# The loads of v for seven of eight batches move from SyncE's queue to GpSimd's

## The chip, the cores and the metric

The kernel runs on one core of one Trainium2 chip. Its time is the device time of one execution in microseconds (us), the median of several. Engines are called as in the profile: PE is TensorE (PEld its loading of weights), DVE is VectorE, ACT is ScalarE, POOL is GpSimd and SP is SyncE. PEq, SPq and so on are the sequencers of these engines, which issue DMAs and wait for semaphores.

## The reference

For each of 8 batches there are u and v (3200 x 256) and z (3200 x 64), all float32:

```
scores = (z @ z.T) / 3200
x      = u * (max(scores, 0)**2 @ v)
gate   = sigmoid(causal 5-tap convolution of x along the rows, one filter per column)
out    = (gate * (x @ w_val)) @ w_out
```

The scores are 3200 x 3200 per batch and symmetric. The weights w_val and w_out (256 x 256) and the taps (5 x 256) come as 64-bit floats and are made into 32-bit ones by the kernel.

## The kernel before

**Precision.** TensorE works in float32r. Each factor is split into a high and a low part, and a product is three matmuls: low x high, high x low, high x high. v too is split: `v_high` (line 410) casts a loaded piece, on ScalarE for all batches but the first, and `v_low` (line 415) subtracts the high part from the loaded piece on DVE. Both parts go to tiles `v_hl0` to `v_hl12`, one for each pair of row tiles (the 25 tiles of 128 rows make 12 pairs and a single). Each of these has one buffer, so the parts for a batch are written as the batch before has used them for the last time.

**Order of the work.** A batch (b = 0 to 7) is cut into six chunks of 512 query rows, and a remainder of 128 rows that is handled beside the sixth chunk (c = 5). For a chunk, 13 steps run over the pairs of key tiles; the sixth has 16, three of them for the remainder. A step's `scores` are computed three steps ahead of their use (AHEAD = 3). `weights_of` then makes the step's weights: ScalarE applies relu (line 640) and square (641) and casts the high part `ah` (643), DVE subtracts for the low part `al` (649). `attend` multiplies them with v on TensorE (line 428, tiles `acc`). Because the scores are symmetric, many blocks are not computed twice: DVE turns a finished block into a tile `turned` (520, 530), `keep` (542) stores it to DRAM as `mir`, and `m_fetch` (551, 555) loads it later as `m`, six steps before its use. Such a step needs no scores; ScalarE only casts `m` to `ah`.

**What sets the order.** The order is written out by hand. A function is hung on a step by `at_step`, and the instructions of each engine run in just the order in which the program emits them. An engine starts each as soon as its semaphores allow, and may be several steps ahead of another engine. An engine's DMAs stand in that engine's order too: a DMA that waits for its buffer holds up everything behind it on the engine that issues it. On SyncE each DMA waits also for an earlier one, as its eight completion semaphores go round.

**The loads of v.** `v_rows` issues four DMAs, one for each 32-partition block, for up to four neighbouring row tiles; `v_load` calls it. For b > 0, the list `V_LOAD` says at which step of the last chunk of the batch before which tiles are loaded, and into which buffer:

```
V_LOAD = (
    (2, (0, 1, 2, 3), (0, 0)), (3, (24,), (1, 6)), (4, (4, 5, 6, 7), (0, 4)),
    (6, (8, 9, 10, 11), (1, 0)), (8, (12, 13), (1, 4)), (10, (20, 21, 22, 23), None),
    (12, (14, 15, 16, 17), None), (16, (18, 19), None),
)
```

The third item is a place in one of two `v_raws` tiles, which share the two buffers of `turned`; `None` means a `v_raw` tile of a ring of two. Tiles 14 to 17 need two calls of `v_rows`, so a batch has nine groups of four DMAs. In this text the row-24 group is the second, which loads the single tile 24, and the ninth group is the one at step 16, tiles 18 and 19; step 16 is the first step of the next batch. The ninth group takes the `v_raw` buffer of tiles 20 to 23, and so must wait until `v_low` of the pair 22, 23 has read it. `V_HIGH` names the step at which each pair is cast; the pair 18, 19 comes last, two steps after its load is issued.

**GpSimd's own work.** It sets or copies the four rows that the convolution needs from the chunk before (`x_halo`, lines 766 and 768), keeps the last four of a chunk (`halo_keep`, 774 and 779), and has a few instructions for the remainder rows (`one_mul`, 1048, and others). These are small and lie between the places where v is loaded.

**The end.** After the last step the remainder of the last batches and the last chunk are finished, TensorE waits there for other engines in turn.

Of the kernel before, what the change touches and what calls it, by code (L numbers as in the profile page):

```python
# [17 lines left out]
def attn_glu_kernel(  # L18
# [29 lines left out]
    nc = tc.nc  # L48
# [303 lines left out]
    def v_rows(dst, b, g, t, m):  # L352

        for a in range(P // BLK):
            k = firsts[g] * P + (a * sizes[g] + t) * BLK
            nc.sync.dma_start(  # L356
                dst[a * BLK : (a + 1) * BLK], v[b, k : k + m * BLK, :].rearrange("(t r) d -> r t d", r=BLK)
            )

    def v_load(b, tiles_, into=None):  # L360


        raw = sb.tile([P, CW // P, D], F32, name="v_raw", bufs=2) if into is None else into
        for j, k in enumerate(tiles_):
            v_raw[b, k] = raw, j
        j = 0
        while j < len(tiles_):
            g, t = homes[tiles_[j]]
            m = 1
            while j + m < len(tiles_) and homes[tiles_[j + m]] == (g, t + m):  # L370
                m += 1
            v_rows(raw[:, j : j + m], b, g, t, m)
            j += m
# [1048 lines left out]
    with tc.manual_schedule():  # L1422
# [13 lines left out]
        for s in range(min(todo), END + 1):  # L1436
            b, c, i = steps[s] if s >= 0 else (0, 0, 0)
# [85 lines left out]
            if s == END:  # L1523

                b, c = LAST
# [93 lines left out]
```

## Time and profile before

| | |
|---|---|
| median of 3 runs | 2260.3 us (2259.65 to 2263.69) |
| the profiled execution's own time | 2260.35 us |
| its span | 2258.3 us |
| granted TensorE clock | 1.00 |
| busy: PE / PEld / DVE / ACT / POOL | 2247.2 / 1943.2 / 1851.7 / 1702.5 / 75.5 us |
| mean DMA traffic | 171 GB/s |
| DMA issues on line 356 (v loads) | 288 |

The span is the time from the first to the last instruction that the profile shows; the execution's time is a little longer. An engine's busy time is the time covered by its instructions. Register work, semaphore waits and issuing of DMAs are not in it. The chain that ended last is followed back from the last instruction, at each step to what released it. A row of waits names who waited, for whom, and then the total, the number of times and the longest. A row of the timeline starts with its start and its length in us, and ends with the idle time of the engine ahead of it and what ended that.

### The profile page before, as it was taken

How to read it: one execution, taken by the hardware profiler on the slowest of the kernel's cores; microseconds unless marked ns; L12 is line 12 of the kernel's file. 1: busy time of each engine (PE TensorE's matmuls, PEld its weight loads, DVE VectorE, ACT ScalarE, POOL GpSimd, SP SyncE). 2: the span in 40 equal slices, each digit the busy share in tenths (PEclk: the TensorE clock that was granted, in tenths of full speed). 3: DMA queues.
4: the chain of work that ended last, by engine and by line, in shares of the span. 5: the costliest groups of instructions: out<-in, count | busy, mean ns of one | idle time of the engine just before them, and what ended most of it. 6: DMA issues, size and time to landing. Idle time of an engine off the chain costs nothing.

```text
span 2258.3 us, 49991 instructions
## 1 busy us (share of the span) xinstructions
PE 2247.2 (100%) x20269; PEld 1943.2 (86%) x20269; DVE 1851.7 (82%) x2292; ACT 1702.5 (75%) x2126; POOL 75.5 (3%) x116
## 2 busy tenths in 40 slices
PE   9999999999999999999999999999999999999998
PEld 7888988889888998888988899888898889988887
DVE  8877788877889778887888868888788887888776
ACT  8987698766887668876598766977669776687753
POOL 0000000000000000000000000000000000000000
PEclk9999999999999999999999999999999999999999
DMA  5556967878677785787767777678777787777672
GB/s 126 118 136 149 211 153 163 191 180 209 150 167 180 187 205 141 177 189 189 180 162 169 186 188 178 160 178 186 187 176 176 166 187 187 176 175 165 168 184 91
DMA packets 700567, 386.59 MB, mean 171 GB/s; under 512 B 411824, under 2 KB 635056, under 8 KB 700336
## 3 DMA queue, kind: packets, MB, share of 16 engines
q1 hardware_dynamic: 699008, 383.01, 71.9%
q8 instruction: 158, 2.59, 0.5%
q14 instruction: 73, 0.60, 0.1%
q10 hardware_dynamic: 1328, 0.39, 0.1%
HBM read 211.82 MB, written 171.44 MB: 170 GB/s over the span
## 4 chain that ended last, share of the span: by engine, by line
PE 95%; DMA 2%; DVE 1%; SPq 1%; issue 1%; ACT 1%; DVEq 0%; ACTq 0%
PE acc L428 69%; PE s L428 13%; PE misc L428 11%; DMA m<-mir 1%; PE acc L725 1%; DVE al L649 1%; SPq L356 1%; DMA v_raws<-in_v_dram 0%; ACT ah L643 0%; SPq L1008 0%; PE misc L435 0%; DVE x L756 0%; SPq L555 0%; PE acc L936 0%; PE misc L936 0%
## 5 line engine op out<-in xcount | busy, mean ns | idle before, releaser
L428 PE MATMUL acc<-ah,v_hl 64*128 64x512 f32 x9472 | 1622.1, 388 | 1.4 <-DVE x L756 0.5
L428 PEld LDWEIGHTS acc<-ah,v_hl 64*128 64x128 f32 x9472 | 967.9, 184 | 148.7 <-issue 2.1
L428 PE MATMUL acc<-al,v_hl 64*128 64x512 f32 x4736 | 979.7, 387 | 1.2 <-DVE al L649 1.1
L428 PEld LDWEIGHTS acc<-al,v_hl 64*128 64x128 f32 x4736 | 496.3, 184 | 73.6 <-DVE al L649 3.2
L649 DVE TENSOR_TENSOR al<-a,ah 128x1024 fp32r<-128x1024 f32 (+1 forms) x346 | 397.0, 1148 | 185.1 <-ACT ah L643 183.4
L640 ACT ACTIVATE a<-s 128x1024 f32<-128x1024 f32 (+1 forms) x346 | 333.2, 963 | 143.5 <-PE s L428 127.9
L643 ACT CAST ah<-m 128x1024 fp32r<-128x1024 f32 x254 | 265.0, 1047 | 141.9 <-PE acc L428 98.4
L641 ACT ACTIVATE a<-a 128x1024 f32<-128x1024 f32 (+1 forms) x346 | 347.7, 1005 | 11.0
L649 DVE TENSOR_TENSOR al<-m,ah 128x1024 fp32r<-128x1024 f32 x254 | 307.5, 1211 | 45.9 <-ACT ah L643 43.4
L643 ACT CAST ah<-a 128x1024 fp32r<-128x1024 f32 (+1 forms) x323 | 319.9, 990 | 10.2
L520 DVE STREAM_TRANSPOSE turned<-a 128x1024 f32<-128x1024 f32 (+1 forms) x278 | 318.4, 1145 | 0.1
L807 DVE SCALAR_TENSOR_TENSOR gate<-x,cw,gate 128x512 f32<-128x512 f32 x384 | 282.4, 735 | 3.6
L428 PE MATMUL s<-zq,zhl 64*128 64x512 f32 (+1 forms) x1596 | 222.8, 378 | 0.2 <-DVE gv L1029 0.2
L428 PEld LDWEIGHTS s<-zq,zhl 64*128 64x128 f32 x1596 | 154.1, 184 | 27.4 <-DVE gv L1029 0.6
L756 DVE TENSOR_TENSOR x<-acc,ut 128x512 f32<-128x512 f32 x96 | 61.9, 686 | 84.8 <-PE acc L428 70.9
L812 ACT ACTIVATE gate<-gate 128x512 f32<-128x512 f32 x96 | 60.6, 631 | 68.2 <-DVE gate L807 68.0
L877 ACT CAST gvh<-gv 128x512 fp32r<-128x512 f32 x96 | 59.4, 620 | 41.4 <-DVE gv L873 41.3
L428 PE MATMUL misc<-xh,w_val_lo 64*128 64x512 f32 x376 | 79.2, 386 | 0.0
L428 PE MATMUL misc<-xl,w_val_hi 64*128 64x512 f32 x376 | 79.2, 386 | 0.0
L428 PE MATMUL misc<-xh,w_val_hi 64*128 64x512 f32 x376 | 79.2, 386 | 0.0
L428 PE MATMUL s<-v_hl,ah 64*128 64x512 f32 x400 | 77.1, 394 | 0.0
L873 DVE TENSOR_TENSOR gv<-misc,gate 128x512 f32<-128x512 f32 x94 | 64.5, 686 | 15.1 <-PE misc L428 10.8
(175 smaller groups left out, 2023.6 us busy)
## 6 DMA issues: line engine op xcount, KB each, us to landing
mir<-turned SPq DMA_DIRECT2D x460, 256.0 KB, 4.1
m<-mir SPq DMA_DIRECT2D x230, 512.0 KB, 4.8
u_raw<-in_u_dram SPq DMA_DIRECT2D x384, 64.0 KB, 3.6
mir<-turned SPq DMA_DIRECT2D x376, 64.0 KB, 2.1
m<-mir SPq DMA_DIRECT2D x94, 256.0 KB, 4.3
out_dram<-ob SPq DMA_DIRECT2D x152, 128.0 KB, 3.1
v_raws<-in_v_dram SPq DMA_DIRECT2D x100, 128.0 KB, 3.8
z_raw<-in_z_dram SPq DMA_DIRECT2D x182, 64.0 KB, 3.2
```

What stands on the lines that cost most here:

```text
L356: nc.sync.dma_start(dst[a * BLK : (a + 1) * BLK], v[b, k : k + m * BLK, :].rearrange("(t r) d -> r t d", r=BLK))
L428: ins = nc.tensor.matmul(out_, st[r], mv[r], start=first, stop=last)
L520: nc.vector.transpose(into[:, t : t + m], a[:, j * w : (j + m) * w].rearrange("p (t m x) -> p t m x", t=m, x=BLK))
L640: nc.scalar.activation(a[:, : n * w].rearrange("p (j x) -> p j x", j=2), s[:, :, :each], AF.Relu, scale=scale)
L641: nc.scalar.activation(a, a, AF.Square)
L643: nc.scalar.copy(hi, a)
L649: nc.vector.tensor_tensor(lo, a, f32(hi), op=ALU.subtract)
L756: nc.vector.tensor_tensor(x[:, h, HALO : HALO + w], accs[b, c][h][:, :w], ut[b, c][:, h, :w], op=ALU.mult)
L807: nc.vector.scalar_tensor_tensor(g, tap, cw[:, h, k : k + 1], g, op0=ALU.mult, op1=ALU.add)
L812: nc.scalar.activation(g, g, AF.Sigmoid)
L873: nc.vector.tensor_tensor(gv[:, :w], pvs[b, c][e][:, :w], gates[b, c][:, e, :w], op=ALU.mult)
L877: nc.scalar.copy(gvs[b, c][0][:, e, :w], gv_[b, c, e][:, :w])
```

## The change

For b > 0 the DMAs of `v_rows` are issued by GpSimd, for b = 0 by SyncE as before. Their places in the program, their sources, their buffers and their sizes stay. There are 4 x 9 of them for each of 7 batches.

```
     def v_rows(dst, b, g, t, m):
 
         for a in range(P // BLK):
             k = firsts[g] * P + (a * sizes[g] + t) * BLK
-            nc.sync.dma_start(
+            (nc.gpsimd if b else nc.sync).dma_start(
                 dst[a * BLK : (a + 1) * BLK], v[b, k : k + m * BLK, :].rearrange("(t r) d -> r t d", r=BLK)
             )
```

More of the change, by code (lines that the diff above doesn't have):

```diff
@@ L355, in v_rows @@
             k = firsts[g] * P + (a * sizes[g] + t) * BLK
-            nc.sync.dma_start(
+            (nc.gpsimd if b else nc.sync).dma_start(
                 dst[a * BLK : (a + 1) * BLK], v[b, k : k + m * BLK, :].rearrange("(t r) d -> r t d", r=BLK)
```

## The prediction

> **What bounds the kernel now.** I read the page's head first, then the span in three stretches, then who waits for whom, then the chain through the one place where TensorE stood still. First the page:
>
> ```profile
> span 2258.3 us, 49991 instructions
> ...
> PE 2247.2 (100%) x20269; PEld 1943.2 (86%) x20269; DVE 1851.7 (82%) x2292; ACT 1702.5 (75%) x2126; POOL 75.5 (3%) x116
> ...
> PE 95%; DMA 2%; DVE 1%; SPq 1%; issue 1%; ACT 1%; DVEq 0%; ACTq 0%
> ```
>
> TensorE is busy for 2247.2 of 2258.3 us and carries 95% of the chain that ended last. Where the missing 11.1 us lie decides what any change off TensorE can give. The stretches (columns: length, then busy time and count by engine, granted clock, DMA share, GB/s):
>
> ```profile
> 0.00:15.00 15.00, 13.06 (x73) 9.03 (x75) 9.92 (x18) 9.26 (x14) 1.32 (x10) 1.00 0.63 136
> 15.00:2220.00 2205.00, 2202.00 (x20018) 1907.54 (x20016) 1817.13 (x2226) 1681.64 (x2087) 72.31 (x102) 1.00 0.74 174
> 2220.00:2258.30 38.30, 32.17 (x184) 26.62 (x180) 24.66 (x50) 11.56 (x26) 1.86 (x4) 0.99 0.14 45
> ```
>
> 1.9 us are lost at the start and 6.1 at the end, where no moved load lies (the first batch keeps SyncE, and nothing is loaded for a ninth). Between them TensorE idles for 2205.00 - 2202.00 = 3.0 us, at full clock. So 3.0 us is the most that this change can win; a loss has no such bound.
>
> Who waits around the moved loads (waiting engine, line, released by: total, times, longest):
>
> ```profile
> ACT ah L643 <- DMA m<-mir: 36.9, 28, 4.7
> ACT v_hl L410 <- DMA v_raws<-in_v_dram: 24.8, 7, 4.6
> SPq L356 <- DVE v_hl L415: 48.7, 7, 8.2
> ```
>
> ScalarE waits once per moved batch for a v load, 24.8/7 = 3.5 us, and 28 times for a mirrored block. SyncE stands 48.7/7 = 7.0 us per batch before the last group of a batch (rows 18 and 19), whose buffer DVE has still to read. None of this reaches TensorE except in one place, at b = 4, where the chain reads (start, length, what):
>
> ```profile
> 1103.09 0.43 SPq L356
> ...
> 1103.62 6.46 DMA m<-mir
> ...
> 1110.15 1.05 ACT ah L643
> ...
> 1111.23 1.24 DVE al L649
> ...
> 1112.51 0.49 PE acc L428
> ```
>
> A mirrored block is fetched only after four v loads have been issued (L356). It lands 6.46 us later, ScalarE and DVE split it, and TensorE gets it late.
>
> **The change, part by part.** 36 DMAs per batch, 252 in all, move from SyncE's queue to GpSimd's. Bytes, buffers and the steps of the program stay.
>
> *Removed from SyncE.* The price of an issue there, by tile (min/median/max in ns):
>
> ```profile
> L356 SPq DMA_DIRECT2D v_raws<-in_v_dram x156: 311/430/2107, 14.3 to 1944.6; - x156
> L356 SPq DMA_DIRECT2D v_raw<-in_v_dram x132: 311/426/1932, 3.1 to 1970.2; - x132
> ```
>
> 252 x 0.43 = 108 us of issue time leave SyncE, off TensorE's path nearly everywhere. What counts is the issue just ahead of the late fetch at b = 4, and the same place at b = 5:
>
> ```profile
> 1100.97 2.55 SPq L356 DMA_DIRECT2D v_raws<-in_v_dram  x4
> 1103.62 1.20 SPq L555 DMA_DIRECT2D m<-mir  x2
> ...
> PE acc L428 <- DVE al L649: 0.8, 1, 0.8
> PE acc L428 <- ACT ah L643: 0.5, 1, 0.5
> ...
> PE acc L428 <- DVE al L649: 0.3, 1, 0.3
> ```
>
> The first two rows are SyncE's timeline: four v loads fill 2.55 us straight ahead of the fetch. The others are TensorE's waits from 1050 to 1130 us, 0.8 + 0.5 = 1.3, and from 1360 to 1411 us, 0.3. A fetch 2.6 us earlier covers both, if its transfer is as long as before: **-1.6 us**. If the transfer grows by what the issue saves: 0. I take -1.6, since the wait sits behind an issue, and keep 0 and -3.0 as ends. SyncE's 7.0 us standing per batch moves to GpSimd too. Behind it on SyncE lie stores of turned blocks and of the output, which no engine awaits there, so I count nothing.
>
> *Added to GpSimd: the price of one issue.* No row of this trace shows a DMA issued by GpSimd. The nearest rows are SyncE's 0.43 us above and GpSimd's own instructions (first row grouped by line: busy, mean ns; the second min/median/max):
>
> ```profile
> L1048 POOL TENSOR_TENSOR one_sum<-one_sum,one_f 128x512 f32<-128x512 f32 (+1 forms) x4 | 6.4, 1594 | 122.4 <-DMA one_f<-in_u_dram 122.4
> L774 POOL COPY halo<-x x40: 191/1052/1219, 56.0 to 2189.7; 128x8 f32<-128x8 f32 x40
> ```
>
> Ends: 0.43 and 1.59 us. A copy of eight elements has a median of 1.05 us, so I take g = 1.05 us as an estimate, nearer to GpSimd's rows than to SyncE's. GpSimd has 75.5 us of work in 2258.3; 252 x 1.05 = 265 us more fit by far. What matters is when a group lands.
>
> *The first eight groups of a batch* (32 DMAs). On SyncE they stand in line; on GpSimd only their buffers hold them. At b = 2, SyncE, then ScalarE's first use:
>
> ```profile
> 520.16 1.77 SPq L542 DMA_DIRECT2D mir<-turned  x4
> ...
> 528.08 2.71 SPq L356 DMA_DIRECT2D v_raws<-in_v_dram  x4
> ...
> 532.92 2.01 SPq L356 DMA_DIRECT2D v_raws<-in_v_dram  x4
> ...
> 536.67 0.41 ACT L410 CAST v_hl<-v_raws 128x256 fp32r<-128x256 f32 x1 [2.97 <-DMA v_raws<-in_v_dram]
> ...
> 575.73 0.63 ACT L410 CAST v_hl<-v_raw 128x512 fp32r<-128x512 f32 x1
> ```
>
> The second buffer is free when the stores issued up to 521.9 have landed, about 2 us on, near 524, and the row-24 group, from 532.92 on SyncE, can start there: 9 us earlier. The first v wait of ScalarE goes, 3.0 us here. At g = 1.05 it ends near 524 + 4.2 + 2 = 530; even at 1.59, near 532.4, it beats 536.67. The 28 DMAs from there on end near 524 + 29.4 + 2 = 555 at g = 1.05, near 571 at 1.59; the last of these eight groups is first used at 575.73. TensorE does not wait at this place, so nothing is counted.
>
> *The ninth group* (rows 18 and 19) is the place that decides. Its buffer comes free at the same moment on either queue, and ScalarE uses it soon after. b = 2 (SyncE, ScalarE, DVE's remainder of the next block, TensorE's first use of it), then the time to landing of these four, then b = 1:
>
> ```profile
> 574.27 1.73 SPq L356 DMA_DIRECT2D v_raw<-in_v_dram  x4
> 580.50 0.63 ACT L410 CAST v_hl<-v_raw 128x512 fp32r<-128x512 f32 x1
> 584.27 1.23 DVE L649 TENSOR_TENSOR al<-a,ah 128x1024 fp32r<-128x1024 f32 x1 [1.16 <-ACT ah L643]
> 586.46 0.39 PE L428 MATMUL acc<-al,v_hl 64*128 64x512 f32 x2
> ...
> DMA to landing us min/median/max: 1.8/1.9/2.1
> ...
> 303.30 2.42 SPq L356 DMA_DIRECT2D v_raw<-in_v_dram  x4
> 308.38 0.61 ACT L410 CAST v_hl<-v_raw 128x512 fp32r<-128x512 f32 x1
> 308.51 1.23 DVE L649 TENSOR_TENSOR al<-a,ah 128x1024 fp32r<-128x1024 f32 x1 [1.17 <-ACT ah L643]
> 310.69 0.39 PE L428 MATMUL acc<-al,v_hl 64*128 64x512 f32 x2
> ```
>
> The block is paired with its use by counting writes and uses in program order. On GpSimd the fourth DMA starts 3g after the first and lands g - 0.43 + 2.1 later, so the group is in 4g + 1.67 us after its buffer is free. At b = 2 ScalarE comes 580.50 - 574.27 = 6.23 us after that, at b = 1 5.08 us. Lateness: 4g - 4.56 and 4g - 3.41. ScalarE's next work is the block that TensorE takes with 586.46 - 585.50 = 0.96 us to spare (585.50 is 584.27 + 1.23; 0.95 at b = 1), its thinnest margin in that chunk. With g = 1.05 the group is in time at b = 2 and 0.79 us late at b = 1, less than 0.95: **0 us**. b = 3 to 7 repeat b = 2 nearly to the tenth. At g = 1.59, b = 2 is 1.80 us late, which is the first rival.
>
> *Queued behind the waiting issue on GpSimd* are the halo copy of the last chunk (L779), a memset of x (L766) and a product (L1048). They start up to 10 us later than now. No engine is listed as waiting for the halo copies, and the x they free is written a chunk's end later: 0.
>
> **Sum.** The profiled execution took 2260.35 us, 2.05 more than its span, beside a median of 2260.3, so one basis serves. 2260.35 - 1.6 + 0 = **2258.8 us**.
>
> **Rivals.**
>
> *GpSimd's issues are long, slower.* If each issue has to sit out a DVE instruction, as the eight-element copies seem to do (0.19 us at best, 1.05 at the median), g = 0.43 + 1.23 (the DVE row above) = 1.66. Lateness is 2.08 us at b = 2 and 3.23 at b = 1; past the margin, 1.1 x 6 + 2.3 = 9 us. Time 2260.35 - 1.6 + 9 = 2267.8. It begins at g = 1.38 and passes 0.2% at about 1.56. For it: those copies. Against it: they read SBUF, and an issue may not.
>
> The Trainium skill, SBUF — State Buffer, section "Who interferes with whom", states that descriptors for GpSimd's DMAs cannot be written while DVE runs a copy or cast in a two-port mode, and advises SyncE or ScalarE under such work; a two-input tensor_tensor is said to take only the read side. By that rule the DVE instructions from 574 to 581 us, which are none of these casts, stop no issue and the forecast stands; by the rows of the copies alone it would be 2267.8. This is why this rival has 0.18 and not more.
>
> *The fetch is not sooner, no change.* DMA transfers are the limit at that place (6.46 us in the chain, where all such fetches have a median of 4.8):
>
> ```profile
> m<-mir SPq DMA_DIRECT2D x230, 512.0 KB, 4.8
> ```
>
> Then 2.6 us of earlier issue end in 2.6 us more of transfer, and the time is 2260.4. In this sense the change may not do what it says.
>
> The Trainium skill, DMA: Bandwidth & Descriptors, section "Issuing engines are not separate DMA queues", has all issuers share the same 16 DMA engines, so a second issuer saves sequencer time alone; by that the 2.55 us of issue are the whole gain, which is the forecast, and nothing of the 6.46.
>
> *The fetches land later, slower.* Loads that ran one after another on SyncE now run beside the fetches. One group of four 128 KB loads more in the way of a fetch costs 0.52 MB over 262 GB/s, 2.0 us. Paid only at b = 4 and 5, where TensorE already waits, it is 4; at all seven, 14. The middle, 9, gives 2269. The rate is that of a busy stretch, its last column:
>
> ```profile
> 548.00:556.00 8.00, 8.00 (x80) 7.96 (x79) 7.52 (x12) 5.23 (x8) 0.00 (x0) 1.00 1.09 262
> ```
>
> Against it: GpSimd's groups are issued about 9 us before SyncE's, mostly ahead of the fetches they would meet.
>
> **How the numbers follow.** Forecast 0.45, no change 0.22, long issues 0.18, later fetches 0.08; 0.04 for g between 1.38 and 1.56, which ends between 2258.8 and 2264.9, and 0.03 for something at the span's ends that these rows do not show. A run of this kernel tells 0.2%, 4.5 us, from no change. Faster by more would need 4.5 us where 3.0 are idle: 0.03. Within: 0.45 + 0.22 + 0.04 = 0.71. Slower: 0.18 + 0.08 = 0.26. The range runs from all 3.0 us won, 2257.4, rounded to 2257, to the two slower rivals, 2269. The forecast's own range is 2257.4 to 2260.4.
>
> **What would show it.** GpSimd's DMA instructions: start to start within the ninth group gives g; below 1.38 the forecast holds. ScalarE's wait for the row-24 group (24.8 us) should fall to near nothing, SyncE's 48.7 us to none. TensorE's 1.3 us near 1110 should be gone; if ScalarE still waits 4.7 us for the fetch there, the second rival is right. If ScalarE waits seven times for v_raw at L410 and TensorE idles near 586 us and at the like place of each batch, the first is. If DVE's or ScalarE's own durations change, all of this is wrong.

## The result: 0.8% slower

| | before | after |
|---|---|---|
| median of 4 runs, us | 2260.24 (2259.65 to 2263.69) | 2278.2 (2276.86 to 2283.07) |
| span of the profiled execution, us | 2258.3 | 2281.3 |

The ratio is 1.0077, with a 95% interval of 1.0064 to 1.0089. The forecast of 2258.8 us is wrong, and 2278.2 us lies outside its range. The profiled execution of the changed kernel is the longest of its four, so its rows show somewhat more than the 18 us that the medians show.

The page of the changed kernel, its busy times, GpSimd's DMA queue and a group of GpSimd's:

```profile
PE 2255.6 (99%) x20269; PEld 1925.0 (84%) x20269; DVE 1852.3 (81%) x2292; ACT 1701.4 (75%) x2126; POOL 200.5 (9%) x368
...
q0 software_dynamic: 9856, 22.95, 4.2%
...
L356 POOL DMA_DIRECT2D v_raws<-in_v_dram x140 | 75.7, 547 | 172.8 <-ACT ah L643 48.2
```

GpSimd issues a DMA in 0.547 us, and 22.95 MB have moved to a queue of their own (q0; the row gives packets, MB and share). DVE and ScalarE work as long as before; TensorE is busy 8.4 us longer with the same number of matmuls. The median time from issue to landing of the mirrored blocks has hardly moved, 5.0 us against 4.8 over the whole span; such an average hides this loss.

The middle one of the same three stretches as in the prediction (length, then busy time and count of PE, PEld, DVE, ACT, POOL, granted clock, DMA share, GB/s):

```profile
15.00:2243.00 2228.00, 2210.29 (x20028) 1889.54 (x20026) 1818.89 (x2228) 1681.74 (x2088) 197.29 (x354) 1.00 0.73 172
```

TensorE idles 2.0 us at the start and 6.0 at the end, as before. The interior is 2228 us instead of 2205: TensorE idles 17.7 us there instead of 3.0, and is busy 8.3 us longer. The waits of the changed kernel say who held it up (total, times, longest):

```profile
PE s L428 <- DVE al L649: 15.5, 6, 3.5
...
DVE zz L215 <- DMA z_raw<-in_z_dram: 19.0, 7, 4.0
...
ACT ah L643 <- DMA m<-mir: 70.9, 31, 5.7
...
ACT v_hl L410 <- DMA v_raw<-in_v_dram: 2.8, 3, 1.6
```

The first row, 15.5 us, is new and is most of the 17.7 us of idle time: six stalls of 3.3, 2.1, 2.8, 1.4, 2.4 and 3.5 us, one beside the loads for each of b = 2 to 7. ScalarE's wait for mirrored blocks has doubled from 36.9 us, and DVE waits 19.0 us in seven places for z. One of the seven, 3.3 us, lies at the start and is all that the kernel before had:

```profile
DVE zz L215 <- DMA z_raw<-in_z_dram: 3.3, 1, 3.3
```

The chain of the changed kernel through the stall at b = 2 shows how these belong together (start, length, what):

```profile
542.02 3.10 SPq L161
...
545.17 8.29 DMA z_raw<-in_z_dram
...
553.65 0.13 DVE zz L215
...
554.86 1.23 DVE al L649
...
556.12 0.96 PE s L428 x7
```

Line 161 loads z, here of the sixth chunk, in four DMAs of 128-byte pieces. DVE turns it (`zz`, line 215). Since DVE takes its instructions in order, the low part of a mirrored step (line 649) stands behind the late turning, and TensorE, which needs that part, stands for 3.3 us, from 552.8 to 556.1. In four of the six places the chain runs through the z load like this; at b = 5 and 6 its last long piece is a mirrored block that comes late, with DVE's wait for z beside it (1.8 and 1.6 us). The z load is late twice over. SyncE needs longer to issue its four DMAs, 9.03 us instead of 3.41, and the last one needs 8.29 us to land. SyncE's timeline, first of the changed kernel and then of the kernel before:

```profile
537.94 9.03 SPq L161 DMA_DIRECT2D z_raw<-in_z_dram  x4
```

```profile
539.46 3.41 SPq L161 DMA_DIRECT2D z_raw<-in_z_dram  x4
542.91 2.29 SPq L356 DMA_DIRECT2D v_raws<-in_v_dram  x4
...
558.04 5.08 SPq L356 DMA_DIRECT2D v_raw<-in_v_dram  x8
```

What is beside it is GpSimd. Its timeline in the changed kernel:

```profile
525.40 4.75 POOL L356 DMA_DIRECT2D v_raws<-in_v_dram  x9 [6.69 <-DVE gate L807]
...
539.83 2.91 POOL L356 DMA_DIRECT2D v_raw<-in_v_dram  x5 [0.30 <-DMA v_raws<-in_v_dram]
...
547.42 0.54 POOL L356 DMA_DIRECT2D v_raw<-in_v_dram  x1 [0.38 <-DMA v_raw<-in_v_dram]
580.81 2.12 POOL L356 DMA_DIRECT2D v_raw<-in_v_dram  x4 [32.46 <-ACT ah L643]
```

From 525.4 to 548.0 GpSimd issues the second to eighth group, 28 DMAs, with no break above 2.6 us, and is then idle for 32 us. On SyncE these groups had stood between the fetches and stores of their steps, and reached to 563. So the last three of them now lie on the z load of the sixth chunk. SyncE's four z loads there, before and then after (count, KB each, median us from issue to landing):

```profile
z_raw<-in_z_dram SPq DMA_DIRECT2D x4, 64.0 KB, 5.0
```

```profile
z_raw<-in_z_dram SPq DMA_DIRECT2D x4, 64.0 KB, 10.2
```

The slowest of the four took 5.2 us before and 12.2 after.

The other 8.3 us, TensorE's longer busy time, are the clock. The changed kernel in the 16 us that follow each of the six stalls (columns as in the stretches above):

```profile
556.12:572.12 16.00, 15.99 (x134) 13.82 (x136) 12.28 (x18) 11.15 (x15) 0.00 (x0) 0.89 0.23 39
840.28:856.28 16.00, 16.00 (x134) 13.99 (x136) 12.29 (x18) 11.67 (x17) 0.00 (x0) 0.89 0.38 65
1120.65:1136.65 16.00, 16.00 (x136) 14.64 (x138) 12.29 (x18) 11.42 (x17) 0.00 (x0) 0.90 0.26 45
1403.90:1419.90 16.00, 15.64 (x148) 12.84 (x150) 12.37 (x19) 13.16 (x17) 0.00 (x0) 1.00 0.44 85
1682.99:1698.99 16.00, 15.99 (x134) 14.29 (x136) 12.29 (x18) 11.07 (x16) 0.00 (x0) 0.89 0.46 78
1968.54:1984.54 16.00, 16.00 (x160) 13.59 (x160) 13.40 (x21) 12.39 (x17) 0.00 (x0) 1.00 0.40 63
```

After four of the six stalls the granted clock is below 1, and 134 to 136 matmuls fit in the 16 us; 148 and 160 fit after the other two. (Part of that is that the matmuls of these stretches are not all of one length.) Read in steps of 1 us, the clock goes down to 0.50 and is back after about 3.4 us each time, so 1.7 us of work is lost; four times this is 6.8 of the 8.3 us.

### The profile page after: what moved, and what is told of

Its sections match the earlier page's. It is cut to its first block, busy times and chain, and to the rows that moved or that the text cites. A ratio compares the mean times of both kernels' runs of the same rounds, so it can differ in the third digit from the quotient of the medians.

```text
span 2281.3 us, 50137 instructions
## 1 busy us (share of the span) xinstructions
PE 2255.6 (99%) x20269; PEld 1925.0 (84%) x20269; DVE 1852.3 (81%) x2292; ACT 1701.4 (75%) x2126; POOL 200.5 (9%) x368
## 3 DMA queue, kind: packets, MB, share of 16 engines
q0 software_dynamic: 9856, 22.95, 4.2%
## 4 chain that ended last, share of the span: by engine, by line
PE 93%; DMA 3%; DVE 2%; SPq 1%; issue 1%; ACT 1%; DVEq 0%; ACTq 0%
PE acc L428 68%; PE s L428 12%; PE misc L428 11%; DMA z_raw<-in_z_dram 1%; DMA m<-mir 1%; SPq L161 1%; DVE al L649 1%; PE acc L725 1%; ACT ah L643 0%; SPq L555 0%; PE misc L435 0%; DVE gate L807 0%; DVE x L756 0%; PE acc L936 0%; PE misc L936 0%
## 5 line engine op out<-in xcount | busy, mean ns | idle before, releaser
L428 PEld LDWEIGHTS acc<-ah,v_hl 64*128 64x128 f32 x9472 | 958.0, 184 | 159.2 <-issue 2.1
L428 PEld LDWEIGHTS acc<-al,v_hl 64*128 64x128 f32 x4736 | 491.3, 185 | 79.5 <-DVE al L649 3.2
L643 ACT CAST ah<-a 128x1024 fp32r<-128x1024 f32 (+1 forms) x323 | 319.8, 990 | 10.2
L768 POOL COPY x<-halo 128x8 f32<-128x8 f32 x40 | 20.0, 501 | 941.8 <-DVE gate L807 941.8
L356 POOL DMA_DIRECT2D v_raws<-in_v_dram x140 | 75.7, 547 | 172.8 <-ACT ah L643 48.2
L356 POOL DMA_DIRECT2D v_raw<-in_v_dram x112 | 60.2, 541 | 255.5 <-ACT ah L643 206.8
L428 PE MATMUL s<-v_hl,al 64*128 64x256 f32 x400 | 66.8, 288 | 15.5 <-DVE al L649 15.5
```

The source lines that it names most:

```text
L356: (nc.gpsimd if b else nc.sync).dma_start(dst[a * BLK : (a + 1) * BLK], v[b, k : k + m * BLK, :].rearrange("(t r) d -> r t d", r=BLK))
L428: ins = nc.tensor.matmul(out_, st[r], mv[r], start=first, stop=last)
L643: nc.scalar.copy(hi, a)
```

## The experiments

In the expectations L is the theory that the ninth group lands late, B that GpSimd's groups come in a burst, and P that its larger packets take longer turns on the DMA engines. Edits are shown against the changed kernel.

**The ninth group alone on GpSimd.**

```
-            (nc.gpsimd if b else nc.sync).dma_start(
+            (nc.gpsimd if b and firsts[g] + t == 18 else nc.sync).dma_start(
```

> Only the ninth group (tiles 18 and 19, the one that waits for its buffer) is issued by GpSimd, the other eight by SyncE. Theory P, packets in turn: GpSimd's queue has packets of 4096 bytes (245 ns each), SyncE's have 128 to 2048 bytes, and the DMA engines take one packet of each queue in turn, so SyncE's fetches crawl while GpSimd's queue is full. Here that is so for only some 2 us a batch, where no fetch is urgent: 2259 to 2262 us. Theory B, burst: the v loads are issued some 9 us earlier and close together, and any queue would slow the fetches: the ninth group is not earlier, so the same 2259 to 2262. Theory L, late landing: the ninth group reaches ScalarE late and costs the time: 2268 or more.

Measured: 2260.35 us beside 2262.04 of the kernel before, ratio 0.9995 (0.9982 to 1.0008). The row of waits:

```profile
ACT v_hl L410 <- DMA v_raw<-in_v_dram: 1.2, 3, 0.6
```

ScalarE waits at most 0.6 us for a `v_raw` load, the ninth group among them. L falls, and B and P had both expected this time; the loss is in the first eight groups. One thing more: TensorE's 1.3 us near 1110 are gone in this run, although four v loads still stand on SyncE ahead of that fetch (1100.72, 2.56 us).

**All nine on GpSimd, but the first eight held to their steps.** GpSimd copies one column of the newest `ah` ahead of each group, so it cannot run ahead of ScalarE. Queue, packets, bytes and buffers stay those of the changed kernel.

```
+    def pace(s):
+        mark = sb.tile([P, 1], F32, name="pace", bufs=1)
+        nc.gpsimd.tensor_copy(mark, f32(at[steps[s + AHEAD - 1]][0][:, :1]))
...
+                if tiles_[0] != 18:
+                    at_step(s1 + p, pace, s1 + p)
                 at_step(s1 + p, v_load_at, b, tiles_, place_)
```

> As the changed kernel, all loads by GpSimd, but ahead of each of the first eight groups GpSimd copies one column of the newest ah tile, so that it issues a group only when ScalarE has come to about that step, near the times at which SyncE issued it. Theory P: the packets are as large as before, the fetches beside them still crawl: 2270 to 2285 us, and the z load of the sixth chunk still lands in 6 us or more. Theory B: with the old times back, the old kernel's time: 2259 to 2264.

Measured: 2258.52 us (2257.32 to 2261.79), ratio to the kernel before 0.9986 (0.9976 to 0.9995). GpSimd's timeline at b = 2, where each group now has its own start, and the waits of this run (its line 211 is line 215 of the others, here and in the two later versions that are held):

```profile
533.89 2.18 POOL L356 DMA_DIRECT2D v_raws<-in_v_dram  x4 [0.30 <-issue]
...
547.66 2.19 POOL L356 DMA_DIRECT2D v_raw<-in_v_dram  x4 [0.31 <-issue]
...
553.65 4.22 POOL L356 DMA_DIRECT2D v_raw<-in_v_dram  x8 [0.29 <-issue]
```

```profile
DVE zz L211 <- DMA z_raw<-in_z_dram: 5.8, 7, 3.2
...
ACT ah L643 <- DMA m<-mir: 31.0, 25, 3.8
...
z_raw<-in_z_dram SPq DMA_DIRECT2D x4, 64.0 KB, 7.4
```

The row of TensorE's six stalls is not there any more. So it is the running ahead that costs, and not the queue or its packets as such: the time is what B expected, and P alone is ruled out as the cause. P's second sign did come, though: the four z loads of the sixth chunk still need 7.4 us in the median (last row, 537 to 553 us), between the 5.0 of the kernel before and the 10.2 of the changed one. They are late by less than the schedule has to spare. DVE turns this z at 547.62 us without a wait, at 548.04 in the kernel before and at 553.65 in the changed one. This version is faster than the changed kernel by 0.9% (the quotient of their ratios), and than the kernel before by 0.14%, with an interval that ends close to 1.

**The first eight groups on ScalarE's queue, the ninth on GpSimd's.**

```
-            (nc.gpsimd if b else nc.sync).dma_start(
+            (nc.sync if b == 0 else nc.gpsimd if firsts[g] + t == 18 else nc.scalar).dma_start(
```

> The first eight groups are issued by ScalarE in the same steps, whose queue is a second one beside SyncE's with packets of 1024 bytes (46 ns); the ninth stays with GpSimd. Theory P: small packets take short turns, the z load lands in about 4 us, 2260 to 2266 us, less well if ScalarE's own time (32 issues of 0.45 us a batch) tells. Theory B: ScalarE issues near the old times, 2259 to 2264 too. If a second queue as such is the trouble, whatever its packets: 2270 to 2285.

Measured: 2317.18 us, ratio 1.0239 (1.022 to 1.0259). Its largest new wait:

```profile
ACT ah L643 <- DMA v_raws<-in_v_dram: 52.8, 14, 5.3
```

The cast of line 643 does not read `v_raws`. So ScalarE must have stood at its own issues, until earlier loads had landed, 14 times, and the casts behind them are late. All three expected ranges are missed. That is another cost than the one in question, so the run's time tells nothing of B or P. It shows what a waiting issue costs on an engine that has work behind it.

**One group, tiles 8 to 11, on GpSimd.** These are the four loads that stood ahead of the late fetch near 1103 us.

```
-            (nc.gpsimd if b else nc.sync).dma_start(
+            (nc.gpsimd if b and firsts[g] + t == 8 else nc.sync).dma_start(
```

> Only the group of tiles 8 to 11 is issued by GpSimd, the one that stood ahead of the late fetch at b = 4. The prediction's gain alone: the fetch is issued 2.5 us sooner and TensorE's wait of 1.3 us there goes: 2258.8 us. Theory P: GpSimd's queue is filled for only 2.2 us, about 9 us ahead of that fetch, so 2258 to 2261. Theory B: the same, since one group makes no burst.

Measured: 2259.75 us, ratio 0.9987 (0.9977 to 0.9997). The fetch is issued at 1103.67 us, no earlier than before: z loads stand ahead of it then (1099.76, 3.81 us). TensorE's waits from 1050 to 1130 us are 0.4 us all the same, instead of 1.3. One group alone does no harm, as B and P both expected, and here the gain near 1110 does not come from an earlier fetch.

**The landing measured by itself.** A small kernel that leaves the whole computation out and only loads: SyncE issues z loads in 128-byte pieces, or loads in 1024-byte pieces, alone, beside 24 v loads from GpSimd, or beside the same 24 from ScalarE, each twice, in one execution. Its core:

```
+        for queue in (None, nc.gpsimd, nc.scalar):
+            for load in (by_128, by_1024):
+                for again in range(2):
...
+                    if queue is not None:
+                        stream(queue, big)
+                    load(small)
```

> Only the disputed cost: nothing of the reference is computed, the output but for a corner is left unwritten. SyncE loads eight pieces of 64 KB, once in pieces of 128 bytes (as z is loaded, 32 per DMA engine and load) and once of 1024 bytes (as v is, 4 per engine and load): alone, beside 24 loads of v of 128 KB from GpSimd's queue, and beside the same 24 from ScalarE's queue; each twice. Theory P, a packet of each queue in turn: alone 2 to 3 us to landing for both; beside GpSimd's 4096-byte packets of 245 ns, 32 x 0.26 = 8 us for the 128-byte loads and 4 x 0.29 + 2 = 3 to 4 us for the 1024-byte loads; beside ScalarE's 1024-byte packets of 46 ns, 32 x 0.06 + 2 = 4 us and 2 to 3 us. If the engines share by bytes instead, loads of the same 64 KB are slowed alike, whatever the size of their pieces.

Measured: 198.0 us for all of it. Landing of SyncE's loads, min/median/max in us:

| | alone | beside GpSimd's | beside ScalarE's |
|---|---|---|---|
| 128-byte pieces | 2.0/2.3/2.5 and 1.9/2.3/2.5 | 2.0/4.7/6.6 and 2.0/5.1/6.9 | 3.4/4.3/5.1 and 3.6/4.5/5.4 |
| 1024-byte pieces | 1.8/1.9/2.0, twice | 1.7/3.7/5.0 and 1.9/4.0/5.1 | 2.2/3.4/4.0 and 2.3/3.5/3.8 |

A stream beside it about doubles a load's median landing, whichever queue carries the stream. Beside GpSimd's the slowest landing is another 1.0 to 1.5 us later than beside ScalarE's. P's 8 us for the 128-byte pieces are not reached, and the medians of both sizes grow nearly alike, by 2.4 to 2.8 and by 1.8 to 2.1 us beside GpSimd's: that is nearer to sharing by bytes. In the trace of the changed kernel nearly all bytes of GpSimd's queue go in packets of 4096 bytes, SyncE's in packets of 128 to 2048. The Trainium skill, DMA: Bandwidth & Descriptors, section "Queues, rings and completion order", has each DMA engine take turns between queues packet by packet; larger packets in one queue would then lengthen the waits of the other, and the slowest landings agree with that in sign. Whether the packets that the trace counts are those of the page, no run shows. The difference of 1.0 to 1.5 us is much smaller than the 7.0 us by which the slowest z load of the sixth chunk grew in the changed kernel (12.2 against 5.2, at b = 2).

**The z load two steps later.** The changed kernel, with the turning and splitting of z for the sixth chunk put off, so that DVE comes to it later.

```
-                late = 1 if b == 1 else 0
+                late = 1 if b == 1 else 2 if c == 5 else 0
```

> The changed kernel with one more change: for b of 2 and more, the z of the sixth chunk, loaded in step 6 of the stretch, is turned by DVE two steps later (and its high and low parts are made two steps later). The chain of the changed kernel goes through the slow landing of that z load (8.3 us) and DVE's wait for it. If DVE's wait is what holds TensorE up, most of the loss of b = 2 to 7 goes: 2262 to 2268 us. If the mirrored fetches, which are as late, hold it up as well, little goes: 2270 to 2280.

Measured: 2267.37 us, ratio 1.0036 (1.0022 to 1.0051), clock 1.00. Its waits:

```profile
DVE zz L215 <- DMA z_raw<-in_z_dram: 3.1, 1, 3.1
...
PE acc L428 <- DVE al L649: 3.2, 6, 0.8
...
ACT ah L643 <- DMA m<-mir: 61.2, 25, 6.5
```

DVE's new waits for z and TensorE's long stalls are gone, and with them 2278.2 - 2267.4 = 11 of the 18 us by the medians, 9 by the two ratios, though every group is issued as in the changed kernel. So DVE's wait for z is the path of the greater part. Of the rest the rows show 3.2 us of short waits in six places, and the chain says whose they are. At b = 2 (start, length, what):

```profile
547.52 7.07 DMA m<-mir
...
557.02 1.43 PE acc L428 x10
```

A mirrored block, fetched behind the slow issues of z, lands late, ScalarE and DVE split it, and TensorE gets it late. The chain goes through such a fetch at each of the six places, and through the landing of z at none. How the remainder splits I did not settle.

**Held only ahead of groups 6 to 8.** One copy in a batch, ahead of tiles 20 to 23. Groups 1 to 5 run ahead freely.

```
+                if tiles_[0] == 20:
+                    at_step(s1 + p, pace, s1 + p)
```

> As the changed kernel, but GpSimd is held once a batch, ahead of the sixth group (tiles 20 to 23), until ScalarE has come to that step. Groups 1 to 5 run ahead as before, groups 6 to 8 go near their old times. The z load of the sixth chunk (issued 538 to 547 us at b = 2) then has no v load beside it. Burst theory, with the z load as the main victim: its landing falls from up to 14 us to about 5, DVE waits little for it, and 11 or more of the 18 us go: 2259 to 2267 us. If the mirrored fetches, issued beside groups 3 to 5, are the main victims: 2270 to 2278.

Measured: 2260.38 us beside 2260.88, ratio 0.9997 (0.9987 to 1.0007). Waits, then the DMA traffic from 537 to 553 us:

```profile
DVE zz L211 <- DMA z_raw<-in_z_dram: 3.3, 1, 3.3
...
ACT ah L643 <- DMA m<-mir: 44.3, 19, 5.8
```

```profile
q1 hardware_dynamic: 6516, 3.13, 84.1%
q0 software_dynamic: 212, 0.48, 15.2%
```

The same view of the changed kernel:

```profile
q1 hardware_dynamic: 4521, 2.24, 69.1%
q0 software_dynamic: 632, 1.46, 43.8%
```

With the sixth group back at 549.0 us, GpSimd moves 0.48 instead of 1.46 MB beside the z load, and SyncE moves 3.13 instead of 2.24. The whole loss is gone. The mirrored fetches from 525 to 552 us still land as late as in the changed kernel, 4.2/8.9/12.5 us (min/median/max) against 4.6/8.6/12.2 (before: 3.5/4.9/6.8). The z loads land in 3.6/6.0/8.7, between before (3.8/5.0/5.2) and after (8.3/10.2/12.2), and DVE does not wait for them. So the fetches that groups 1 to 5 make late cost TensorE nothing here.

**Held only ahead of groups 1 to 5.** Groups 6 to 8 run ahead, from 545.7 us on.

```
+                if place_ is not None:
+                    at_step(s1 + p, pace, s1 + p)
```

> The other half: GpSimd is held ahead of each of groups 1 to 5 until ScalarE has come to the step, and groups 6 to 8 follow group 5 at once. They then come some 6 us sooner than in the old kernel, when the z load has been issued. Burst theory: no fetch that is urgent stands beside a close row of v loads, 2257 to 2262 us. If groups 6 to 8 are harmful wherever they run ahead: 2266 or more.

Measured: 2269.49 us beside 2260.88, ratio 1.0038 (1.0025 to 1.0051). The burst theory's 2257 to 2262 is missed, the other branch, 2266 or more, is met. The waits, then the chain at b = 3 (start, length, what):

```profile
DVE zz L211 <- DMA z_raw<-in_z_dram: 10.4, 10, 3.2
...
PE s L428 <- DVE gv L1029: 4.9, 6, 1.7
...
ACT ah L643 <- DMA m<-mir: 73.8, 40, 4.4
```

```profile
829.49 12.32 DMA m<-mir
...
841.91 1.06 ACT ah L643
...
844.22 0.61 DVE gv L1029
...
844.87 0.96 PE s L428 x6
```

Groups 6 to 8 running ahead are enough for 0.38% of the 0.77%, also when those before them keep their places. But the path is not that of z: DVE waits for z by at most 1.4 us at once beside these loads, and the chain does not go through its landing. At five of the six places its longest piece is a mirrored fetch of 10.2 to 13.3 us, which makes ScalarE, DVE and then TensorE late. With the run before: it is these three groups that must be kept back, for the sake of the z load and of the mirrored fetches beside them.

## Why the prediction was wrong

**The step that failed** is in the part on the first eight groups: "TensorE does not wait at this place, so nothing is counted." I asked only when these groups land against their own first use. They are in time, and ScalarE's wait for `v_raws` is gone as forecast. I had worked out that they would start 9 us earlier and did not ask what they would meet there. So the cost of the loads beside them was put at nothing; measured, it is the 18 us, since the same loads held to their steps cost none. On SyncE the v loads stood in line with the other loads, and at b = 2 the last three of the eight groups were issued from 553.2 us on, 10 us and more after the z load. GpSimd has little in its way (at b = 2 it never waits more than 2.6 us on an earlier load), and it issued them in one burst onto the z load and the fetches beside it. DVE turns z in its place in the order, and the low part that TensorE waits for stands behind it.

**The later-landing rival** had the right kind of mechanism and a chance of 0.08. It named the mirrored fetches as what suffers. They do suffer: with z out of the way, or with groups 1 to 5 held, the chain goes through a late fetch, and the kernel loses 6.6 and 8.6 us against the one before. But they are the second victim, the z load is the first, and the fetches are late without harm when the last three groups are held. Its argument against itself, that GpSimd's groups lie "mostly ahead of the fetches they would meet", was the mistake at its root: earlier than one neighbour is beside another. Its 9 us were the middle between 4 and 14, from the bytes of one group, so that the run with such fetches in its chain loses 8.6 us is luck. The price was 18 us: seven groups follow one another, SyncE's own issues take longer with the landing, and four of the stalls halve the clock, which no term held. No row of the prediction was about z at all.

**The price of an issue**, 1.05 us from GpSimd's small copies, was mis-sized: 0.547 us measured. The range of 0.43 to 1.59 held it. So the ninth group came nearly in time (ScalarE waits 2.8 us for `v_raw` in all, at most 1.6 at once), the long-issue rival was wrong, and the burst was denser than my 29.4 us for 28 DMAs (22.6 us). The copies were no guide to an issue. One sum was loose too: by its own terms b = 1 passes its margin from g = (3.41 + 0.95) / 4 = 1.09 on, not from 1.38; at 0.547 nothing hangs on it. The rule of the Trainium skill, SBUF — State Buffer, section "Who interferes with whom", that I weighed there did not decide anything: the 252 issues took 0.50 to 0.95 us, and none waited out a DVE instruction of 1.23 us. Only one of them ran beside a DVE cast (line 645, at 253.9 us), and it is the longest, 0.95 us. That agrees with the rule, but it is one case.

**The most to win**, 3.0 us of interior idle time, is not contradicted as a bound: the held version's profiled span is 2.3 us shorter than that of the kernel before. Its ratio leaves 1.1 to 5.4 us of gain, too wide to test the bound. **The 1.6 us near 1110** are not shown to come from the earlier fetch. They went also where the v loads stayed ahead of it, and all but 0.4 us went where it was issued no earlier. Each kernel has one profiled execution here, so why is open. **The rival of no change** fell with the result.

**Still open** is whether GpSimd's larger packets add something to the burst in the full kernel; no run had the burst without them. Why SyncE's issues take longer beside the burst is open too. Issuing half of each group from SyncE in the same places was not tried.

## What to carry to other kernels

An in-order queue that stands and waits is also what spaces its transfers; here, moving loads to an idle engine's queue took that spacing away, and they started about as early as their buffers allowed. Before such a move, list what the earlier transfers will lie beside, the most urgent loads first, and follow who waits for those. If the move is wanted all the same, a cheap dependency on the step (here one column copied per group) puts the spacing back.

## What was unexpected of the hardware

The clock: the stall that ends at 840.28 us, 2.10 us long, is followed by the lowered clock, worth 1.7 us; the one that ends at 1968.54, 3.53 us long, is not. TensorE's timeline of the changed kernel at these two places:

```profile
840.28 0.48 PE L428 MATMUL s<-v_hl,al 64*128 64x256 f32 x2 [2.10 <-DVE al L649]
...
1968.54 0.39 PE L428 MATMUL s<-v_hl,al 64*128 64x256 f32 x2 [3.53 <-DVE al L649]
```

The Trainium skill, TensorE: Matmul & The Clock Gate, section "Part 1: The HAM clock gate", tells of a half clock after an idle window of about 3.4 us and of a window that runs free of the kernel. The 3.4 us at half clock agree with that length, and the free window would fit that a stall of 3.5 us escaped; that a stall of 2.10 us was enough does not fit a whole idle window, and the measurement decides. So here each of the stalls of 2.1 to 3.3 us cost 1.7 us more in clock, and those of 1.4 and 3.5 us nothing.

A DMA issued by GpSimd took 0.547 us of it, against SyncE's 0.43, and a stream of v loads beside them about doubled the median landing of small loads, from 2.3 to between 4.3 and 5.1 us.
